# Second mixture of a recurrence and two mixtures of experts: program order on all engines, the input check and the loads spread over its blocks

## The chip, the core and the metric

The program runs on one core of a Trainium2 chip. The time is device microseconds of one execution; three runs of the kernel before gave 1580.2 us as their median (1580.01 to 1581.79). The engines are PE (TensorE matmul; PEld is its weight load), DVE (VectorE), ACT (ScalarE), POOL (GpSimd) and SP (SyncE, which here issues nearly all DMAs).

## The reference, cut to what is computed

```python
# 1. a recurrence over 768 steps, for 4 x 8 heads with a 40 x 40 state
for t in range(S):
    y[:, :, t] = einsum('bhd,bhde->bhe', rt, state)
    Sa = einsum('bhde,bhe->bhd', state, at)
    state = state * wt[:, :, None, :] - einsum('bhd,bhe->bhde', Sa, bt)
    state = state + einsum('bhd,bhe->bhde', vt, kt)
x = y.transpose(0, 2, 1, 3).reshape(3072, 320)
# 2. the first mixture, 1536 wide
x = ((x @ w_a) * (x @ w_b)) @ w_out
# 3. the second mixture, 4 experts, 1024 wide
p = domain_probs / (domain_probs.sum(-1, keepdims=True) + 1e-9)
for e in range(4):
    out += p[:, e:e+1] * (np.maximum(x @ w1[e], 0) @ w2[e])
```

## The kernel before

The program has one long straight run of instructions. The recurrence and the first mixture (class Moe1) are interleaved by hand up to about 853 us of the profile. The second mixture (class Moe2) follows, and this change is about it.

**Blocks.** The 3072 tokens are cut into 6 tiles t of 512. Each of the 4 experts e has 1024 hidden features, in 8 steps k of 128; two sets of weights u (512 features each) serve one expert. The list `steps` of `Moe2.run` runs over e, then t, then k: 192 blocks. Every fp32 operand is split into a high and a low part, so that three matmuls (high by high, high by low, low by high) replace one.

A block has two halves. `Moe2.l1` makes 8 matmuls of 512 columns (L719) into a PSUM tile l; then ACT makes hh, the relu of it rounded (L722), and DVE makes hl, the remainder (L723). `Moe2.l2` makes 12 matmuls of 320 columns (L736 to L738), three for each of the four 128-token groups o of the tile: L736 and L737 read hh, L738 reads hl. At k = 7 DVE adds the four groups o, weighted by the expert's probability, into the accumulator acc (L741); in the last expert the tile then goes to memory (L744). In the program l1 of block j + 1 stands ahead of l2 of block j.

**Loads.** `Moe2.loadx` fetches one token tile (6 DMAs, 768 KB, into a staging tile xB) and splits it: ACT casts each of three pieces to XH (L444), DVE subtracts to XL (L445). `Moe2.weights` fetches one set u (r1, 768 KB, L677, and r2, 640 KB, L679) and splits it: ACT casts, POOL subtracts (L445), and a third piece s goes through ACT and DVE (L687, L688). All staging tiles share one tag "st" with two buffers. The split weights have three buffers.

**The guard.** `Guard.run` checks the inputs of the recurrence while the second mixture runs: 48 chunks g of 419 KB are loaded (L795), ACT copies a part to gw (L797) and squares the rest with a sum (L801), DVE takes a maximum and a minimum of gw (L791). Then 24 parts gx of up to 512 KB of the first mixture's weights are squared by ACT (L810) and reduced by DVE. Its tag "g" has two buffers. `Moe2.run` calls it one step per block, in the program's text. `Guard.close` turns the results into one flag, and the program branches on it at its end to `general`, a slow path not taken here.

**Order.** Up to 853 us PE and SP stand in the order of the program's text. In the second mixture nothing is fixed by hand: a scheduler of the compiler orders each engine's instructions from the dependences, its own cost estimates and free buffers. Every engine then runs its instructions in the order given, and each waits for the semaphores of what it reads and overwrites.

Of the kernel before, what the change touches and what calls it, by code (L numbers as in the profile page):

```python
# [22 lines left out]
N = NPASS * NCH  # L23
# [3 lines left out]
DM = 320  # L27
FF1 = 1536
NE, FF2 = 4, 1024
# [48 lines left out]
class Att:  # L78
# [363 lines left out]
def split(nc, raw, hi, lo, eng):  # L442

    nc.scalar.copy(hi, raw)  # L444
    eng.tensor_tensor(out=lo, in0=raw, in1=hi, op=ALU.subtract)  # L445
# [5 lines left out]
class Moe1:  # L451
# [104 lines left out]
    def run(self):  # L556

        n = self.NK1
        blocks = [(t, i) for t in range(NT // 256) for i in range(n)]
        yield 0  # L560
        for t, i in blocks[:self.AHEAD]:
            yield from self.l1(t, i)
        for j, (t, i) in enumerate(blocks):
            if j + self.AHEAD < len(blocks):
                t1, i1 = blocks[j + self.AHEAD]
                if i1 == 0:
                    yield t1
                yield from self.l1(t1, i1)
            yield from self.l2(t, i)
# [73 lines left out]
class Moe2:  # L643


    TT, NB = 512, NT // 128
    NTT = NT // TT

# [23 lines left out]
        self.acc = self.fix2.tile([128, self.NB, DM], F32, name="acc")  # L672

    def weights(self, u, w1, w2):
        nc, pool = self.nc, self.pool
        r1 = pool.tile([128, 3, 512], F32, tag="st", name=f"r1_{u}")
        nc.sync.dma_start(r1[:], w1)  # L677
        r2 = pool.tile([128, 4, DM], F32, tag="st", name=f"r2_{u}")
        nc.sync.dma_start(r2[:], w2)  # L679
        h1 = pool.tile([128, 2, 512], F32R, tag="h1", name=f"h1_{u}", bufs=3)  # L680
        l1 = pool.tile([128, 2, 512], F32R, tag="l1", name=f"l1_{u}", bufs=3)
        s1 = pool.tile([128, 512], F32R, tag="s1", name=f"s1_{u}", bufs=3)
        h2 = pool.tile([128, 4, DM], F32R, tag="h2", name=f"h2_{u}", bufs=3)
        l2 = pool.tile([128, 4, DM], F32R, tag="l2", name=f"l2_{u}", bufs=3)
        for f in range(2):
            split(nc, r1[:, f], h1[:, f], l1[:, f], nc.gpsimd)
        nc.scalar.copy(s1[:], r1[:, 2])  # L687
        nc.vector.tensor_tensor(out=s1[64:128], in0=r1[64:128, 2], in1=s1[64:128], op=ALU.subtract)  # L688
        for q in range(2):
            k = slice(2 * q, 2 * q + 2)  # L690
            split(nc, r2[:, k], h2[:, k], l2[:, k], nc.gpsimd)
        self.W[u] = h1, l1, s1, h2, l2

    def loadx(self, t, fix):
        nc = self.nc
        XH = fix.tile([128, 3, self.TT], F32R, name=f"XH{t}")
        XL = fix.tile([128, 3, self.TT], F32R, name=f"XL{t}")
        xf = self.pool.tile([128, 3, self.TT], F32, tag="st", name=f"xB_{t}")
        for i in range(2):
            c, x = slice(256 * i, 256 * i + 256), self.x2d[2 * t + i]  # L700
            nc.sync.dma_start(xf[:, 0:2, c], x[:, 0:2])
            for z in range(2):
                nc.sync.dma_start(xf[64 * z:64 * z + 64, 2, c], x[:64, 2])
        for f in range(3):
            split(nc, xf[:, f], XH[:, f], XL[:, f], nc.vector)
        self.X[t] = XH, XL

    def l1(self, u, t, k, name):
        nc, TT = self.nc, self.TT
# [36 lines left out]
    def run(self, w1, w2, out, aside):  # L746

        nc = self.nc
        nc.gpsimd.memset(self.acc[:], 0.0)
        for t in range(1, self.NTT):  # L750
            self.loadx(t, self.fix2)
        steps = [(e, t, k) for e in range(NE) for t in range(self.NTT) for k in range(8)]

        def l1(j):
            e, t, k = steps[j]
            self.l1(2 * e + k // 4, t, k % 4, j)

        l1(0)
        for j, (e, t, k) in enumerate(steps):
            for z in range(2):  # L760
                if (t, k) == ((1, 0), (self.NTT - 1, 4))[z] and e + 1 < NE:
                    u = 2 * e + 2 + z
                    self.weights(u, w1[u], w2[u])
            if j + 1 < len(steps):
                l1(j + 1)
            self.l2(2 * e + k // 4, t, k % 4, j, self.pn[:, :, e], k == 0, k == 7, out if e == NE - 1 else None)
            next(aside, None)


class Guard:  # L770
# [15 lines left out]
    def run(self):  # L786
        nc, st, X = self.nc, self.st, mybir.AxisListType.X
        most, least, size, tiny = (st[:, i] for i in range(4))

        def worst(i, n, src, op):  # L790
            nc.vector.tensor_reduce(out=st[:src.shape[0], i, n:n + 1], in_=src, axis=X, op=op)  # L791

        for n in range(N):
            t = self.pool.tile([128, 1032], F32, tag="g", name=f"g_{n}")[:104]
            nc.sync.dma_start(t, self.e1[n])  # L795
            w = self.pool.tile([128, 256], F32, tag="w", name=f"gw_{n}")[:104]
            nc.scalar.copy(w.rearrange("p (a t) -> p a t", t=32), t[:, :264].rearrange("p (a t) -> p a t", t=33)[:, :, 1:])  # L797
            yield
            worst(0, n, w, ALU.max)
            worst(1, n, w, ALU.min)  # L800
            nc.scalar.activation(t, t, AF.Square, accum_out=size[:104, n:n + 1])  # L801
            yield
        n = 0
        for src in self.words:
            for i in range(0, src.shape[1], self.WORDS):
                m = min(self.WORDS, src.shape[1] - i)
                t = self.pool.tile([128, 1032], U32, tag="g", name=f"gx_{n}")[:, :m]
                nc.sync.dma_start(t, src[:, i:i + m])
                w = self.pool.tile([128, self.WORDS // 2], F32, tag="w", name=f"gy_{n}")[:, :m // 2]
                nc.scalar.activation(w, t.bitcast(F32).rearrange("p (n z) -> p n z", z=2)[:, :, 1], AF.Square)  # L810
                yield
                worst(3, n, w, ALU.min)
                n += 1
                yield

    def close(self, ps):

# [11 lines left out]
def general(tc, e1, e2, cst, wab, w2d, wo, probs, w1, w2, out):  # L829

    nc = tc.nc
    v = nc.vector
    NS = N // SUP
    with ExitStack() as c:
        dram = c.enter_context(tc.tile_pool(name="gdram", bufs=1, space=DRAM))
        x2 = dram.tile([NS, 128, 3, 256], F32, name="x2g")
        with ExitStack() as ctx:
# [5 lines left out]
            pool = ctx.enter_context(tc.tile_pool(name="grec", bufs=2))  # L843
# [19 lines left out]
            def tile4(name):  # L863
                return pool.tile(full, F32, tag=name, name=name)
# [4 lines left out]
            with tc.For_i(0, NS, 1) as s:  # L869
                ys = pool.tile([104, 8, SUP, 32], F32, tag="ys", name="gys", bufs=1)  # L870
                for step in range(2):
# [3 lines left out]
                    for z in range(2):  # L875
                        n = 2 * step + z
                        nc.sync.dma_start(E1[:, z], e1.rearrange("(s c) p m -> s c p m", c=SUP)[bass.ds(s, 1), n].rearrange("o p m -> p (o m)"))
                        src = e2.rearrange("(s c) p m -> s c p m", c=SUP)[bass.ds(s, 1), n].rearrange("o p m -> p (o m)")
                        src = src.rearrange("p (y v j t) -> p y v j t", y=2, v=2, j=4)
# [5 lines left out]
                    for z in range(2):  # L885
                        x = E1[:, z, 264:776].rearrange("p (a y t) -> p a y t", y=2, t=32)
                        for y in range(2):
                            nc.scalar.copy(kb[:, z, y], x[:, :, y])
                    w = E1[:, :, :264].rearrange("p z (a t) -> p z a t", t=33)[:, :, :, 1:]
                    a = E1[:, :, 776:].rearrange("p z (a t) -> p z a t", t=32)  # L890
                    for t in range(31, -1, -1):
                        dr, dv, x, y = (tile4(i) for i in ("gr", "gv", "gx", "gy"))
# [28 lines left out]
        m2 = Moe2(c, tc, x2, probs, None)  # L921
# [2 lines left out]
        nc.sync.dma_start(pd[:].rearrange("e p n -> p n e"), m2.pn[:])  # L924
        v.memset(m2.acc[:], 0.0)
        for t in range(m2.NTT):
            m2.loadx(t, m2.fix2)
        with tc.For_i(0, NE, 1) as e:
            for u in range(2):
                m2.weights(u, *(x.rearrange("(e u) p a b -> e u p a b", u=2)[bass.ds(e, 1), u].rearrange("o p a b -> (o p) a b") for x in (w1, w2)))  # L930
            p = m2.pool.tile([128, m2.NB], F32, tag="p", name="gp")
            nc.sync.dma_start(p[:], pd[bass.ds(e, 1)].rearrange("o p n -> (o p) n"))
            for t in range(m2.NTT):
                for k in range(8):
                    m2.l1(k // 4, t, k % 4, (t, k))
                    m2.l2(k // 4, t, k % 4, (t, k), p, k == 0, k == 7, None)
# [4 lines left out]
def body(ctx, tc, e1, e2, vt, cst, wab, w2d, wo, probs, w1, w2, out):  # L941
    nc = tc.nc
# [5 lines left out]
    with ExitStack() as ca:  # L948
# [41 lines left out]
        def whole(g):  # L990
            for _ in g:
                pass
# [10 lines left out]
        v, pool = nc.vector, nc.gpsimd  # L1003
# [126 lines left out]
        for n in range(SUP, N):  # L1130
            s, cc = divmod(n, SUP)
            m = n + LEAD
            g = (28, 20) if n < RING else (44, 28)
# [55 lines left out]
        hand.close()  # L1189
        cb.close()  # L1190
        m2 = Moe2(late, tc, x2d, probs, "right")
        m2.weights(0, w1[0], w2[0])
        m2.loadx(0, m2.fix)
        m2.weights(1, w1[1], w2[1])
        moe(1 << 20)
    m2.second()
    guard = Guard(late, tc, e1, (wab, w2d, wo))
    m2.run(w1, w2, out, guard.run())
    other = guard.close(m2.ps1.tile([128, 512], F32, tag="l1", name="other"))
    late.close()  # L1200
    with tc.If(other != 0):
# [53 lines left out]
```

## Time and profile before

| | |
|---|---|
| median of three runs | 1580.2 us |
| the profiled execution's own time | 1580.34 us |
| its span, first to last instruction | 1578.2 us |
| second mixture on PE | 853 to 1571 us of the span |
| busy over the span: PE, PEld, DVE, ACT, POOL | 90%, 82%, 53%, 37%, 27% |

The span is 2.1 us shorter than the execution's own time, and the profiled execution lies 0.1 us above the median. The page cuts the span into 40 slices of 39.5 us; the second mixture fills slices 22 to 40. From the row of PE alone they all look alike. The rows of PEld, ACT and of the DMAs differ between slices 22 to 27 (the guard's stretch, roughly 865 to 1075 us) and the rest.

### The profile page before, as it was taken

What the parts mean: (1) busy time and instruction counts of PE and PEld (TensorE: products, weight loads), DVE (VectorE), ACT (ScalarE), POOL (GpSimd) and SP (SyncE); (2) the same over time, 40 slices, a digit from 0 to 9 for tenths busy, and PEclk for the clock granted to TensorE, in tenths of its full rate; (3) what the DMA queues carried; (4) which work ended last, traced back from release to release, by engine and by line L of the source; (5) the groups of instructions that cost most, each with busy time, mean ns of one, the idle gap of its engine ahead of it and who ended that gap; (6) DMA issues with size and microseconds to landing.
All of it is one profiled execution on the core that took longest, in us unless ns stands there. A gap on an engine that the chain in (4) does not pass through costs nothing.

```text
span 1578.2 us, 40657 instructions
## 1 busy us (share of the span) xinstructions
PE 1427.1 (90%) x17202; PEld 1296.1 (82%) x17202; DVE 837.0 (53%) x1663; ACT 581.7 (37%) x1426; POOL 428.5 (27%) x810
## 2 busy tenths in 40 slices
PE   3455579999999999999999999999999999999998
PEld 2455568898898898898899877788999899989997
DVE  7658987777677677764445444553222322222222
ACT  2233334544544544543345766542112211121111
POOL 7083856246246246246013100020001100010000
PEclk9956679999999999999999999999999999999999
DMA  7745233443443443532124855671001100000001
GB/s 178 205 125 162 48 68 99 102 98 93 107 92 94 108 94 91 110 76 56 49 91 133 221 145 145 172 257 40 1 0 38 38 1 0 1 1 29 22 18 36
DMA packets 146850, 135.85 MB, mean 86 GB/s; under 512 B 98852, under 2 KB 116708, under 8 KB 146660
## 3 DMA queue, kind: packets, MB, share of 16 engines
q1 hardware_dynamic: 140468, 124.72, 30.4%
q10 hardware_dynamic: 6192, 8.45, 1.7%
q8 instruction: 137, 2.24, 0.6%
q14 instruction: 53, 0.43, 0.1%
HBM read 115.03 MB, written 18.09 MB: 84 GB/s over the span
## 4 chain that ended last, share of the span: by engine, by line


## 5 line engine op out<-in xcount | busy, mean ns | idle before, releaser
L723 DVE SCALAR_TENSOR_TENSOR hl<-l,hh 128x512 fp32r<-128x512 f32 x192 | 132.3, 689 | 344.1 <-ACT hh L722 344.0
L586 PE MATMUL l<-xh,w 128*128 128x256 f32 x1440 | 293.7, 289 | 12.1 <-DVE g L590 6.5
L722 ACT ACTIVATE hh<-l 128x512 fp32r<-128x512 f32 x192 | 114.0, 594 | 396.6 <-PE l L719 396.5
L586 PE MATMUL l<-xl,w 128*128 128x256 f32 x864 | 246.1, 292 | 5.9 <-DVE xl L445 5.7
L586 PEld LDWEIGHTS l<-xh,w 128*128 128x128 f32 x1440 | 237.7, 194 | 15.5 <-DVE g L590 7.1
L736 PE MATMUL o<-h,hh 128*128 128x320 f32 x768 | 238.9, 311 | 9.2 <-ACT hh L722 5.8
L738 PE MATMUL o<-h,hl 128*128 128x320 f32 x768 | 239.6, 313 | 4.6 <-DVE hl L723 4.5
L737 PE MATMUL o<-l,hh 128*128 128x320 f32 x768 | 236.9, 309 | 0.0
L218 POOL TENSOR_TENSOR tmp<-tblk,xblk 128x126 f32<-128x126 f32 (+22 forms) x341 | 141.1, 414 | 269.9 <-DMA tblk<-td 164.3
L445 POOL TENSOR_TENSOR l<-r,h 128x512 fp32r<-128x512 f32 (+1 forms) x32 | 47.0, 1490 | 577.5 <-ACT h L444 577.5
L586 PEld LDWEIGHTS l<-xl,w 128*128 128x128 f32 x864 | 167.6, 194 | 9.9 <-DVE xl L445 8.2
L736 PEld LDWEIGHTS o<-h,hh 128*128 128x128 f32 x768 | 144.2, 188 | 25.6 <-ACT hh L722 13.6
L221 POOL TENSOR_TENSOR xblk<-xblk,tmp 128x126 f32<-128x126 f32 (+22 forms) x341 | 152.0, 446 | 26.7
L738 PEld LDWEIGHTS o<-h,hl 128*128 128x128 f32 x768 | 144.0, 188 | 11.3 <-DVE hl L723 11.0
L719 PE MATMUL l<-XL,h 128*128 128x512 f32 x384 | 151.7, 395 | 0.0
L719 PE MATMUL l<-XH,h 128*128 128x512 f32 x384 | 151.6, 395 | 0.0
L719 PE MATMUL l<-XH,l 128*128 128x512 f32 x384 | 149.9, 390 | 0.0
L737 PEld LDWEIGHTS o<-l,hh 128*128 128x128 f32 x768 | 144.2, 188 | 6.7
L597 ACT CAST gh<-g 128x256 fp32r<-128x256 f32 x144 | 58.4, 406 | 157.4 <-DVE g L590 153.4
L174 PE MATMUL psT<-A,e 40*64 40x32 f32 x1472 | 63.6, 240 | 39.8 <-POOL A L154 12.3
L588 ACT COPY a<-l 128x256 f32<-128x256 f32 x144 | 53.5, 372 | 123.0 <-PE l L586 121.7
L174 PEld LDWEIGHTS psT<-A,e 40*64 40x64 f32 x1472 | 58.0, 158 | 43.6 <-issue 24.0
(122 smaller groups left out, 2628.0 us busy)
## 6 DMA issues: line engine op xcount, KB each, us to landing
g<-e SPq DMA_DIRECT2D x48, 419.2 KB
e<-e SPq DMA_DIRECT2D x46, 419.2 KB
e<-e SPq DMA_DIRECT2D x48, 208.0 KB
tblk<-td SPq DMA_DIRECT2D x96, 64.0 KB
r<-w SPq DMA_DIRECT2D x8, 768.0 KB
gx<-wab SPq DMA_DIRECT2D x12, 512.0 KB
r<-w SPq DMA_DIRECT2D x8, 640.0 KB
G<-vt SPq DMA_DIRECT2D x96, 52.0 KB
```

The costliest lines, as they stand in the source:

```text
L174: nc.tensor.matmul(T[P][KROW[P]:KROW[P] + 64, a], ke[r, a].rearrange("p y t -> p (y t)"), self.A[P][r, k, a], start=True, stop=True)
L218: eng.tensor_tensor(out=t, in0=tb[:, k + 1:, k:k + 1].to_broadcast([128, m, c]), in1=X[:, k:k + 1, :c].to_broadcast([128, m, c]), op=ALU.mult)
L221: eng.tensor_tensor(out=X[:, k + 1:, :c], in0=X[:, k + 1:, :c], in1=t, op=ALU.subtract)
L586: nc.tensor.matmul(o, l, r, start=j == 0, stop=j == len(ops) - 1)
L588: nc.scalar.copy(a[:], ps[:, 0:256])
L597: self.nc.scalar.copy(gh[:], g[:])
L719: nc.tensor.matmul(ps[:], l, r, start=i == 0, stop=i == len(ops) - 1)
L722: nc.scalar.activation(hh[:], ps[:], AF.Relu)
L723: nc.vector.scalar_tensor_tensor(out=hl[:], in0=ps[:], scalar=0.0, in1=hh[:], op0=ALU.max, op1=ALU.subtract)
L736: nc.tensor.matmul(o[:], hh[:, s], h2[:, k], start=first, stop=False)
L737: nc.tensor.matmul(o[:], hh[:, s], lo2[:, k], start=False, stop=False)
L738: nc.tensor.matmul(o[:], hl[:, s], h2[:, k], start=False, stop=last)
```

## The change

The diff, cut to its core. `LAND` is the number of blocks between the issue of a load and the first instruction that reads it. `weights` and `loadx` become generators, which are advanced one step after each block; `whole` runs one to its end at once, for the first two sets of weights and the first token tile. The slow path `general` does the same in loops and is left out here.

```diff
+    LAND = 3
...
     def weights(self, u, w1, w2):
-        r1 = pool.tile([128, 3, 512], F32, tag="st", name=f"r1_{u}")
+        r1 = pool.tile([128, 3, 512], F32, tag="st", name=f"r1_{u}", bufs=4)
...
+        for _ in range(self.LAND):
+            yield
         for f in range(2):
             split(nc, r1[:, f], h1[:, f], l1[:, f], nc.gpsimd)
+            yield
         nc.scalar.copy(s1[:], r1[:, 2])
...
         for q in range(2):
+            yield
             k = slice(2 * q, 2 * q + 2)
             split(nc, r2[:, k], h2[:, k], l2[:, k], nc.gpsimd)
...
     def loadx(self, t, fix):
...
+        for _ in range(self.LAND):
+            yield
         for f in range(3):
             split(nc, xf[:, f], XH[:, f], XL[:, f], nc.vector)
+            yield
...
     def run(self, w1, w2, out, aside):
-        for t in range(1, self.NTT):
-            self.loadx(t, self.fix2)
         steps = [(e, t, k) for e in range(NE) for t in range(self.NTT) for k in range(8)]
+        begin = {8 * t - 8: [self.loadx(t, self.fix2)] for t in range(1, self.NTT)}
+        for e in range(NE - 1):
+            for z in range(2):
+                u = 2 * e + 2 + z
+                begin[8 * self.NTT * (e + 1) - 8 + 4 * z] = [self.weights(u, w1[u], w2[u])]
...
+        going = []
         l1(0)
         for j, (e, t, k) in enumerate(steps):
-            for z in range(2):
-                if (t, k) == ((1, 0), (self.NTT - 1, 4))[z] and e + 1 < NE:
-                    u = 2 * e + 2 + z
-                    self.weights(u, w1[u], w2[u])
+            going += begin.pop(j, [])
             if j + 1 < len(steps):
                 l1(j + 1)
             self.l2(2 * e + k // 4, t, k % 4, j, self.pn[:, :, e], k == 0, k == 7, out if e == NE - 1 else None)
-            next(aside, None)
+            going = [g for g in going if next(g, going) is not going]
+            if j >= 8:
+                next(aside, None)
...
+        def chunk(n):
             t = self.pool.tile([128, 1032], F32, tag="g", name=f"g_{n}")[:104]
             nc.sync.dma_start(t, self.e1[n])
+            yield
             w = self.pool.tile([128, 256], F32, tag="w", name=f"gw_{n}")[:104]
             nc.scalar.copy(w.rearrange("p (a t) -> p a t", t=32), t[:, :264].rearrange("p (a t) -> p a t", t=33)[:, :, 1:])
             yield
             worst(0, n, w, ALU.max)
             worst(1, n, w, ALU.min)
             nc.scalar.activation(t, t, AF.Square, accum_out=size[:104, n:n + 1])
...
+        jobs = [chunk(n) for n in range(N)] + [part(n, src) for n, src in enumerate(parts)]
+        next(jobs[0])
+        for i, job in enumerate(jobs):
+            if i + 1 < len(jobs):
+                next(jobs[i + 1])
+            for _ in job:
+                yield
+            yield
...
-    m2.run(w1, w2, out, guard.run())
+    with tc.manual_schedule(engines={getattr(mybir.EngineType, x) for x in ("PE", "SP", "DVE", "Pool", "Activation")}):
+        m2.run(w1, w2, out, guard.run())
```

So `run` now stands on all five engines in the order of its text. Token tile t is issued at block 8t - 8 and split at blocks 8t - 5 to 8t - 3; its first reader is l1 in block 8t - 1's turn. The weights of the next expert are issued 8 and 4 blocks before its first block and split over five turns from the third on. The guard starts at block 8, takes two blocks for each chunk or part, and issues each load two blocks before its copy; 72 chunks and parts take 144 blocks.

The order on ACT where the guard runs, before: `g_15` is chunk 15 of the guard and `gw_15` its copied part, `hh_16` is the relu of block 16.

```order
L797 COPY gw_15_15620<-g_15_15618 104x256
L801 ACTIVATE g_15_15618,gst_14596<-g_15_15618 104x1032
L722 ACTIVATE hh_16_15159<-l1_16_15150 128x512
L797 COPY gw_16_15685<-g_16_15683 104x256
L801 ACTIVATE g_16_15683,gst_14596<-g_16_15683 104x1032
L797 COPY gw_17_15742<-g_17_15740 104x256
L722 ACTIVATE hh_17_15191<-l1_17_15182 128x512
L801 ACTIVATE g_17_15740,gst_14596<-g_17_15740 104x1032
L797 COPY gw_18_15799<-g_18_15797 104x256
L801 ACTIVATE g_18_15797,gst_14596<-g_18_15797 104x1032
```

The same blocks on ACT now:

```order
L731 ACTIVATE hh_15_15042<-l1_15_15033 128x512
L810 COPY gw_3_15060<-g_3_14999 104x256
L731 ACTIVATE hh_16_15071<-l1_16_15062 128x512
L814 ACTIVATE g_3_14999,gst_14596<-g_3_14999 104x1032
L731 ACTIVATE hh_17_15103<-l1_17_15094 128x512
L810 COPY gw_4_15134<-g_4_15058 104x256
L731 ACTIVATE hh_18_15145<-l1_18_15136 128x512
```

Between two relus stood two or three of the guard's instructions, chunk 15 and on at block 16; now one stands there, and chunk 3 is at hand.

The order on ACT where the second mixture begins, before: `x2_11` is the last result tile of the first mixture, `XH1` and `XH2` are the split token tiles 1 and 2, `hh_0` the first relu.

```order
L636 COPY x2_11_14569<-o01_11_14242 128x512
L637 COPY x2_11_14569<-o2_11_14243 64x256
L444 CAST XH1_14603<-xB_1_14605 128x512 x3
L444 CAST XH2_14618<-xB_2_14620 128x512 x3
L722 ACTIVATE hh_0_14687<-l1_0_14678 128x512
```

The same place now:

```order
L636 COPY x2_11_14569<-o01_11_14242 128x512
L637 COPY x2_11_14569<-o2_11_14243 64x256
L731 ACTIVATE hh_0_14614<-l1_0_14605 128x512
L731 ACTIVATE hh_1_14627<-l1_1_14618 128x512
L731 ACTIVATE hh_2_14665<-l1_2_14656 128x512
```

The six casts that stood ahead of the first relu have moved behind it, to blocks 3 to 5 and 11 to 13.

The order of DMA issues on SP where the next expert's weights `r1_2`, `r2_2` stand, before:

```order
L795 DMA g_2_14834<-e1 104x1032
L677 DMA r1_2_14927<-w1 128x1536
L795 DMA g_3_14891<-e1 104x1032
L679 DMA r2_2_14929<-w2 128x1280
L795 DMA g_4_14975<-e1 104x1032
```

And now:

```order
L807 DMA g_16_15811<-e1 104x1032
L679 DMA r1_2_15876<-w1 128x1536
L681 DMA r2_2_15878<-w2 128x1280
L807 DMA g_17_15885<-e1 104x1032
L807 DMA g_18_15942<-e1 104x1032
```

The weights have moved back from the guard's third chunk (L795) to its seventeenth (now L807), and one set's two transfers stand together.

## Rows read from the trace of the kernel before

**Rows 1.** Page: two engines' busy tenths in 40 slices of the span.

```profile
PE   3455579999999999999999999999999999999998
PEld 2455568898898898898899877788999899989997
```

**Rows 2.** Stretches: PE, PEld, DVE, ACT, POOL busy (count), PEclk, DMA share, GB/s.

```profile
870.00:1063.00 193.00, 179.47 (x930) 149.80 (x929) 95.32 (x194) 118.63 (x227) 17.43 (x12) 1.00 0.65 185
...
1083.00:1276.00 193.00, 193.00 (x1073) 174.55 (x1072) 52.02 (x83) 37.58 (x64) 11.32 (x8) 1.00 0.05 16
```

**Rows 3.** Waits in 870 to 1063: total us, times, longest us.

```profile
ACT gw L797 <- DMA g<-e: 48.5, 46, 2.4
...
PEld o L736 <- ACT hh L722: 13.1, 18, 1.2
PEld o L738 <- DVE hl L723: 10.5, 24, 0.6
```

**Rows 4.** Waits in 1083 to 1560, first row of the same view.

```profile
ACT hh L722 <- PE l L719: 376.5, 129, 3.0
```

**Rows 5.** Timeline in the guard's stretch: start us, us, engine, operation [idle before].

```profile
933.13 0.41 ACT L797 COPY gw<-g 104x256 f32<-104x256 f32 x1 [1.52 <-DMA g<-e]
...
933.57 1.07 ACT L801 ACTIVATE g<-g 104x1032 f32<-104x1032 f32 x1
...
935.58 0.41 ACT L797 COPY gw<-g 104x256 f32<-104x256 f32 x1 [0.85 <-DMA g<-e]
...
936.02 1.07 ACT L801 ACTIVATE g<-g 104x1032 f32<-104x1032 f32 x1
...
937.08 0.58 ACT L722 ACTIVATE hh<-l 128x512 fp32r<-128x512 f32 x1
...
937.71 0.41 PE L736 MATMUL o<-h,hh 128*128 128x320 f32 x1 [0.41 <-ACT hh L722]
...
938.44 0.41 PE L738 MATMUL o<-h,hl 128*128 128x320 f32 x1 [0.17 <-DVE hl L723]
```

**Rows 6.** Timeline, one undisturbed block after the guard, ACT, DVE and PE.

```profile
1149.88 0.60 ACT L722 ACTIVATE hh<-l 128x512 fp32r<-128x512 f32 x1 [2.99 <-PE l L719]
...
1150.51 0.69 DVE L723 SCALAR_TENSOR_TENSOR hl<-l,hh 128x512 fp32r<-128x512 f32 x1 [2.90 <-ACT hh L722]
...
1153.27 0.30 PE L736 MATMUL o<-h,hh 128*128 128x320 f32 x1
...
1153.56 0.31 PE L738 MATMUL o<-h,hl 128*128 128x320 f32 x1
```

**Rows 7.** Timeline of SP's queue, issues of two loads.

```profile
830.11 0.35 SPq L679 DMA_DIRECT2D r<-w  x1
...
864.72 0.50 SPq L795 DMA_DIRECT2D g<-e  x1
```

**Rows 8.** Timeline of ACT, the first instructions that read those loads.

```profile
834.60 1.36 ACT L444 CAST h<-r 128x640 fp32r<-128x640 f32 x2 [0.40 <-DMA r<-w]
...
869.64 0.41 ACT L797 COPY gw<-g 104x256 f32<-104x256 f32 x1 [2.42 <-DMA g<-e]
```

**Rows 9.** Timeline, all engines, the first blocks of the second mixture.

```profile
854.48 0.47 SPq L640 DMA_DIRECT2D x<-x  x1
...
856.80 0.39 PE L719 MATMUL l<-XH,h 128*128 128x512 f32 x1
...
857.28 1.09 ACT L722 ACTIVATE hh<-l 128x512 fp32r<-128x512 f32 x2
...
857.93 0.41 PE L736 MATMUL o<-h,hh 128*128 128x320 f32 x1
```

**Rows 10.** Groups in 870 to 1063: count | busy us, mean ns | idle before.

```profile
L791 DVE TENSOR_REDUCE gst<-gw 104x1 f32<-104x256 f32 x96 | 35.8, 414 | 55.1 <-ACT gw L797 54.9
...
L741 DVE SCALAR_TENSOR_TENSOR acc<-o,pn,acc 128x320 f32<-128x320 f32 x24 | 11.8, 542 | 0.0
```

**Rows 11.** Timeline of PE, the larger of two waits late in the first mixture.

```profile
833.81 0.38 PE L586 MATMUL l<-xh,w 128*128 128x256 f32 x1 [0.22 <-DVE g L590]
```

More of the change, by code (lines that the diff above doesn't have):

```diff
@@ L675, in weights @@
         nc, pool = self.nc, self.pool
-        r1 = pool.tile([128, 3, 512], F32, tag="st", name=f"r1_{u}")
+        r1 = pool.tile([128, 3, 512], F32, tag="st", name=f"r1_{u}", bufs=4)
         nc.sync.dma_start(r1[:], w1)
-        r2 = pool.tile([128, 4, DM], F32, tag="st", name=f"r2_{u}")
+        r2 = pool.tile([128, 4, DM], F32, tag="st", name=f"r2_{u}", bufs=4)
         nc.sync.dma_start(r2[:], w2)
@@ L684, in weights @@
         l2 = pool.tile([128, 4, DM], F32R, tag="l2", name=f"l2_{u}", bufs=3)
+        for _ in range(self.LAND):
+            yield
         for f in range(2):
             split(nc, r1[:, f], h1[:, f], l1[:, f], nc.gpsimd)
+            yield
         nc.scalar.copy(s1[:], r1[:, 2])
         nc.vector.tensor_tensor(out=s1[64:128], in0=r1[64:128, 2], in1=s1[64:128], op=ALU.subtract)
+        self.W[u] = h1, l1, s1, h2, l2
         for q in range(2):
+            yield
             k = slice(2 * q, 2 * q + 2)
             split(nc, r2[:, k], h2[:, k], l2[:, k], nc.gpsimd)
-        self.W[u] = h1, l1, s1, h2, l2
     def loadx(self, t, fix):
@@ L697, in loadx @@
         XL = fix.tile([128, 3, self.TT], F32R, name=f"XL{t}")
-        xf = self.pool.tile([128, 3, self.TT], F32, tag="st", name=f"xB_{t}")
+        xf = self.pool.tile([128, 3, self.TT], F32, tag="st", name=f"xB_{t}", bufs=4)
         for i in range(2):
@@ L703, in loadx @@
                 nc.sync.dma_start(xf[64 * z:64 * z + 64, 2, c], x[:64, 2])
+        self.X[t] = XH, XL
+        for _ in range(self.LAND):
+            yield
         for f in range(3):
             split(nc, xf[:, f], XH[:, f], XL[:, f], nc.vector)
-        self.X[t] = XH, XL
+            yield
     def l1(self, u, t, k, name):
@@ L791, in worst @@
             nc.vector.tensor_reduce(out=st[:src.shape[0], i, n:n + 1], in_=src, axis=X, op=op)
-        for n in range(N):
+        def chunk(n):
             t = self.pool.tile([128, 1032], F32, tag="g", name=f"g_{n}")[:104]
             nc.sync.dma_start(t, self.e1[n])
+            yield
             w = self.pool.tile([128, 256], F32, tag="w", name=f"gw_{n}")[:104]
@@ L801, in run, with part @@
             nc.scalar.activation(t, t, AF.Square, accum_out=size[:104, n:n + 1])
+        def part(n, src):
+            t = self.pool.tile([128, 1032], U32, tag="g", name=f"gx_{n}")[:, :src.shape[1]]
+            nc.sync.dma_start(t, src)
             yield
[L803 to L810, printed above, removed]
+            w = self.pool.tile([128, self.WORDS // 2], F32, tag="w", name=f"gy_{n}")[:, :src.shape[1] // 2]
+            nc.scalar.activation(w, t.bitcast(F32).rearrange("p (n z) -> p n z", z=2)[:, :, 1], AF.Square)
+            yield
+            worst(3, n, w, ALU.min)
+        parts = [src[:, i:min(i + self.WORDS, src.shape[1])] for src in self.words for i in range(0, src.shape[1], self.WORDS)]
+        jobs = [chunk(n) for n in range(N)] + [part(n, src) for n, src in enumerate(parts)]
[4 more added lines that the diff above has]
+            for _ in job:
                 yield
-                worst(3, n, w, ALU.min)
-                n += 1
-                yield
+            yield
     def close(self, ps):
@@ L926, in general @@
         for t in range(m2.NTT):
-            m2.loadx(t, m2.fix2)
+            for _ in m2.loadx(t, m2.fix2):
+                pass
         with tc.For_i(0, NE, 1) as e:
             for u in range(2):
-                m2.weights(u, *(x.rearrange("(e u) p a b -> e u p a b", u=2)[bass.ds(e, 1), u].rearrange("o p a b -> (o p) a b") for x in (w1, w2)))
+                for _ in m2.weights(u, *(x.rearrange("(e u) p a b -> e u p a b", u=2)[bass.ds(e, 1), u].rearrange("o p a b -> (o p) a b") for x in (w1, w2))):
+                    pass
             p = m2.pool.tile([128, m2.NB], F32, tag="p", name="gp")
@@ L1191, in body @@
         m2 = Moe2(late, tc, x2d, probs, "right")
-        m2.weights(0, w1[0], w2[0])
-        m2.loadx(0, m2.fix)
-        m2.weights(1, w1[1], w2[1])
+        whole(m2.weights(0, w1[0], w2[0]))
+        whole(m2.loadx(0, m2.fix))
+        whole(m2.weights(1, w1[1], w2[1]))
         moe(1 << 20)
```

## The prediction

> **What bounds the kernel now.** I read the page first. In its slices PE shows nines from the seventh slice to the last but one, so by that row the second mixture is full everywhere; PEld falls to 7 in slices 24 to 26 [rows 1]. So I cut the second mixture into two stretches of the same 193 us and counted matmuls: 930 from 870 to 1063, 1073 from 1083 to 1276 [rows 2]. Both run the same 20 matmuls per block, at a granted clock of 1.00, its 2.4 GHz level. The second stretch takes 193 / 1073 = 0.180 us for one, 3.60 us for a block. At that pace 930 matmuls take 930 x 0.180 = 167.3 us, so the first stretch loses **25.7 us**.
>
> The view of waits says where. In the first stretch weight loads wait for the relu hh on ACT 13.1 us and for hl on DVE 10.5 us, together 23.6 of the 25.7 us; ACT itself waits 48.5 us, in 46 places, for the guard's loads [rows 3]. In 1083 to 1560 the longest entry is the other way round, ACT waits for PE [rows 4]; no entry of that view has PE waiting. The timeline shows the mechanism: from 933.13 to 937.08 ACT does two copies and two squares of the guard, with a wait of 0.85 us for a load between them, and only then the relu; PE waits for that relu and, 0.7 us later, for hl [rows 5]. ACT is not full there (118.6 of 193 us, [rows 2]); it is in the wrong order, since a copy that has to wait for a load stands ahead of a relu.
>
> PE's idle time alone would size this wrongly: 193 - 179.5 = 13.5 us [rows 2]. The Trainium skill, Perfetto Trace Analysis, section Identifying the Most-Contended Engine, says that matmul busy time is no measure of headroom and that the busy time of weight loads is. By that rule the loss would be (174.55 - 149.80) / 0.904 = 27.4 us and the time 1.7 us lower than mine; the trace sides with it against the 13.5 us, since the count gives 25.7.
>
> **The change, part by part.**
>
> *The guard spread out.* Work is the same; it is done over 144 blocks (some 518 us) instead of about 200 us. In the worst block ACT has the relu 0.60, a square 1.07 with its short read-out, and one cast; its sum is about 0.6 + 1.1 + 0.7 = 2.4 us of the 3.60 [rows 5, 6], the cast being half of a pair of 1.36 [rows 8]. The wait that the change adds is the copy's on its load, and behind it on ACT stand the next relu, then hl on DVE, then PE. Its cover: a load can be issued when the square two jobs earlier is through, and its copy comes three blocks later, less the square: 3 x 3.60 - 1.2 = 9.6 us. The guard's load took 4.9 us from issue (864.72) to the copy that waited for it (869.64) [rows 7, 8]. Past 9.6 us ACT waits, but uses first its own idle 2.99 - 0.41 = 2.6 us before the next relu, then the margin of hl: done at 1151.20, read at 1153.56, 2.36 us [rows 6]. So a load may take 9.6 + 2.6 + 2.4 = 14.6 us before PE feels it. I take 0 for these waits.
>
> *Weights and token tiles.* They are issued three turns, 10.8 us, ahead of their first cast. A 640 KB load took 4.5 us, from 830.11 to 834.60 [rows 7, 8]; behind a 768 KB one at the same rate 4.5 x 2.2 = 9.9 us, but r2 is first read after two more turns. A guard load that follows a whole set on SP is held by its buffer for two blocks anyway. SP itself is held by nothing else: four staging buffers instead of two mean that no issue waits for a split. For both together I take **+0.5 us** of new waits, between 0 (rows above) and 6 us (one us lost at each of the six weight sets, which would need loads three times as long).
>
> *DVE at a tile's end.* hl 0.69, four additions to acc of 0.54 [rows 6, 10] and two reductions of 0.41 make 3.7 us in one block of 3.60, with a lighter one before and after; the next hl slips by under 1 us, against 2.36 of margin. The first group o is free some 0.7 + 0.54 us after hl begins, and its next writer comes after eight more matmuls, so it costs nothing. If that cover were gone, each tile's end would lose up to 0.5 us (a rival below).
>
> *The order of PE.* In the undisturbed stretch the built order of PE was l1 of one block, l2 of the one before, as it is now written. So from there to the end nothing changes, and the last block and the output keep their place.
>
> *The beginning.* The first relu waits for the store of the first mixture's last tile, whose memory it takes (issued 854.48); it ran at 857.28, behind six casts, and PE began l2 at 857.93 [rows 9]. The casts are gone from there, the store is not. Before, PE filled the time from 856.80 with four matmuls of block 2; written in the text's order it has nothing to fill with. The loss is up to 857.93 - 856.80 = 1.1 us, and 0.2 more for hl. If the store lands early, there is a gain of 0.3. I take **+0.8 us**, between -0.3 and +1.3, since the relu began right at the casts' end and the store is the nearer bound.
>
> *The end of the first mixture.* Four staging buffers let the loads of the first two weight sets go out earlier, and on ACT the casts of the first token tile move up by two instructions. PE waits twice there, 0.22 us the longer [rows 11]. I take 0, between -1 and +1.
>
> The sum, on the profiled execution: 1578.2 - 25.7 + 0.5 + 0.8 = 1553.8 us of span, with the 2.1 us around it 1555.9; the median lies 0.1 us lower: **1555.8 us**.
>
> **The rivals.**
>
> *Loads at the expert's change.* ACT stands in the text's order behind a load that is late, because guard, r1 and r2 share one queue. For it: the stretch of before moves 185 GB/s at a DMA share of 0.65 [rows 2], so loads there are already slowed by each other. Against it: the new traffic is one guard load of 0.43 MB in 7.2 us and six sets more, far less. One us for each of six sets: 1561.8.
>
> *DVE at tile ends.* The 3.7 us in a block of 3.60 eat the margin. For it: DVE in order cannot put hl ahead of acc. Against: 2.36 us [rows 6]. At 18 tile ends with guard work, 0.5 us each: 1555.8 + 9 = 1564.8.
>
> *No change.* The slow pace belongs to the DMA traffic or to shared memory, not to the order, and the guard carries it along into later blocks. For it: only the stretch with traffic is slow. Against: the two waits on ACT and DVE already hold 23.6 of 25.7 us [rows 3]. Time: 1580.
>
> *Slower.* The guard's loop on ACT closes on itself: square, issue, landing, copy, next square. Once a load takes over 14.6 us, every further us is lost in each round of two jobs, 36 rounds. From 15.3 us the whole gain is given back, at 16 us the time is 1555.8 + 36 x 1.4 = 1606. Against it: 4.9 us [rows 7, 8].
>
> **How the numbers follow.** Forecast 0.73, loads 0.12, DVE 0.06, no change 0.05, slower 0.04. The range takes the bounds of the sum: at the low end no new waits (-0.5), the beginning at -0.3 (-1.1), the end of the first mixture at -1 and about a us of small waits just outside the stretch, 1552; at the high end 6 us of new waits (+5.5), the beginning at +1.3 (+0.5) and +1, 1563. That holds the forecast and most of the first rival, some 0.83. A measurement of this kernel tells about 0.2% (3 us) from no change: faster 0.91, within it 0.05, slower 0.04.
>
> **What would show it.** Right: in the new trace a stretch of 193 us from 870 on has about 1073 matmuls and over 174 us of weight loads; ACT waits for the guard's loads in no block after the first; the guard's last reduction lies near block 152, about 1400 us; PE still waits about a us at its first l2. Wrong: waits of PE for hh around 1000 to 1026, 1172 to 1198 or 1345 to 1371 (loads at the expert's change); for hl or o every eighth block (DVE); a matmul pace below 0.180 us each without waits (traffic); copies of the guard that wait each time (the loop).

## The result and the profile after

| | before | after |
|---|---|---|
| median, five runs each | 1581.8 us (1580.0 to 1583.2) | 1556.3 us (1554.1 to 1558.4) |
| profiled execution | 1580.3 us | 1556.4 us |
| its span | 1578.2 us | 1554.6 us |

The ratio is 0.9832, with a 95% interval from 0.9815 to 0.9849. The change makes the kernel faster by some 1.7%; the forecast was 1555.8 us.

The page of after has no sevens left in the row of PEld after the first slices but for the last one, where [rows 1] had a dip in slices 24 to 26:

```profile
PE   3445679999999999999999999999999999999998
PEld 2444569998998998998899899999999999999997
```

The two stretches of [rows 2], now of after (busy us and count of PE, PEld, DVE, ACT and POOL, then the granted clock, the DMA share and GB/s):

```profile
870.00:1063.00 193.00, 193.00 (x1075) 174.68 (x1074) 76.38 (x147) 78.08 (x152) 11.46 (x8) 1.00 0.30 81
1083.00:1276.00 193.00, 193.00 (x1076) 174.79 (x1075) 69.25 (x135) 69.40 (x133) 11.46 (x8) 1.00 0.28 81
```

They have become alike. The first went from 930 matmuls to 1075, and ACT's 118.6 us of work there became 78.1, with most of the rest in the second stretch (37.6 before, 69.4 now).

The waits of the whole second mixture, 853 to 1555 us (total us, times, longest us):

```profile
ACT hh L731 <- PE l L728: 469.6, 190, 3.9
...
ACT hh L731 <- DMA x<-x: 2.6, 1, 2.6
...
PEld o L745 <- ACT hh L731: 0.8, 1, 0.8
...
PEld o L747 <- DVE hl L732: 0.4, 1, 0.4
PE o L745 <- ACT hh L731: 0.3, 1, 0.3
...
PE o L747 <- DVE hl L732: 0.2, 1, 0.2
```

The relu's line is now L731, the three matmul lines of l2 are L745 to L747. What [rows 3] held is gone: no entry has ACT waiting for a load of the guard, where there were 48.5 us. The waits of PE for hh and hl that are left have the count 1 each, and all four are at the first l2. ACT waits for PE, as in [rows 4] in the undisturbed part.

ACT's timeline in the same part of the program as [rows 5] (start us, us, engine, operation, idle before):

```profile
928.25 0.60 ACT L731 ACTIVATE hh<-l 128x512 fp32r<-128x512 f32 x1 [2.70 <-PE l L728]
928.75 0.61 ACT L444 CAST XH<-xB 128x512 fp32r<-128x512 f32 x1
929.25 1.07 ACT L814 ACTIVATE g<-g 104x1032 f32<-104x1032 f32 x1
...
931.85 0.60 ACT L731 ACTIVATE hh<-l 128x512 fp32r<-128x512 f32 x1 [1.43 <-PE l L728]
932.34 0.61 ACT L444 CAST XH<-xB 128x512 fp32r<-128x512 f32 x1
932.85 0.41 ACT L810 COPY gw<-g 104x256 f32<-104x256 f32 x1
```

One guard instruction and one cast stand between two relus, and the copy at 932.85 has no idle time before it: its load had landed. The relus follow each other in 3.60 us.

**The second mixture alone.** The first matmul of the second mixture and its last one bound the changed part. For before and for after they are, in PE's timeline:

```profile
853.05 0.40 PE L719 MATMUL l<-XH,h 128*128 128x512 f32 x1
...
1570.51 0.31 PE L738 MATMUL o<-h,hl 128*128 128x320 f32 x1
```

```profile
854.78 0.40 PE L728 MATMUL l<-XH,h 128*128 128x512 f32 x1
...
1546.84 0.31 PE L747 MATMUL o<-h,hl 128*128 128x320 f32 x1
```

From one to the other it is 717.46 us before and 692.06 after, so the change is worth 25.40 us there. The tail behind it is 7.7 us in both. The part ahead came out 1.7 us later, which gives the span's 23.6. That part hardly differs in any kernel of this study, yet its end lies between 851.3 and 855.7 us over eleven profiled executions; so single us of the whole time say little, and the experiments are read by this distance, called the **PE distance** below.

| kernel | PE distance | time | ratio to before, 95% |
|---|---|---|---|
| before | 717.46 us | 1581.8 us | 1 |
| after | 692.06 | 1556.3 | 0.9832 (0.9815 to 0.9849) |
| e1, before's text in fixed order | 708.45 | 1570.2 | 0.9935 (0.9912 to 0.9959) |
| e2, after's text without fixed order | 717.46 | 1580.1 | 0.9991 (0.9979 to 1.0003) |
| e3, before without the guard | 691.27 | 1557.5 | 0.9855 (0.9832 to 0.9878) |
| e4, LAND = 0 | 691.97 | 1555.6 | 0.9832 (0.9803 to 0.9860) |
| e5, two guard steps per block | 692.05 | 1554.0 | 0.9822 (0.9793 to 0.9850) |
| e6, three guard steps per block | 730.13 | 1592.9 | 1.0067 (1.0040 to 1.0094) |
| e7, one guard buffer | 692.06 | 1556.8 | 0.9839 (0.9811 to 0.9868) |
| e8, l1 two blocks ahead | 690.99 | 1554.2 | 0.9835 (0.9806 to 0.9863) |
| e9, one buffer and two steps | 803.55 | 1664.8 | one run |

Each ratio is taken against runs of before from the same round, whose medians are 1581.8 (after), 1581.2 (e1, e2, e3, e8) and 1582.2 us (e4 to e7).

### The profile page after: what moved, and what is told of

Read it like the earlier page. It is cut to its first block, busy times and chain, and to the rows that moved or that the text cites. A ratio compares the mean times of both kernels' runs of the same rounds, so it can differ in the third digit from the quotient of the medians.

```text
span 1554.6 us, 40653 instructions
## 1 busy us (share of the span) xinstructions
PE 1416.2 (91%) x17202; PEld 1299.7 (84%) x17202; DVE 830.4 (53%) x1663; ACT 574.3 (37%) x1426; POOL 424.6 (27%) x810
## 4 chain that ended last, share of the span: by engine, by line
## 5 line engine op out<-in xcount | busy, mean ns | idle before, releaser
L731 ACT ACTIVATE hh<-l 128x512 fp32r<-128x512 f32 x192 | 114.9, 599 | 472.2 <-PE l L728 469.6
L586 PEld LDWEIGHTS l<-xh,w 128*128 128x128 f32 x1440 | 240.3, 196 | 14.6 <-ACT xh L444 6.3
L747 PE MATMUL o<-h,hl 128*128 128x320 f32 x768 | 237.3, 309 | 0.2 <-DVE hl L732 0.2
L745 PE MATMUL o<-h,hh 128*128 128x320 f32 x768 | 236.6, 308 | 0.3 <-ACT hh L731 0.3
L221 POOL TENSOR_TENSOR xblk<-xblk,tmp 128x126 f32<-128x126 f32 (+22 forms) x341 | 148.5, 435 | 26.7
L745 PEld LDWEIGHTS o<-h,hh 128*128 128x128 f32 x768 | 144.2, 188 | 8.3 <-ACT hh L731 0.8
L747 PEld LDWEIGHTS o<-h,hl 128*128 128x128 f32 x768 | 144.2, 188 | 0.4 <-DVE hl L732 0.4
```

The costliest lines, as they stand in the source:

```text
L221: eng.tensor_tensor(out=X[:, k + 1:, :c], in0=X[:, k + 1:, :c], in1=t, op=ALU.subtract)
L586: nc.tensor.matmul(o, l, r, start=j == 0, stop=j == len(ops) - 1)
L731: nc.scalar.activation(hh[:], ps[:], AF.Relu)
L745: nc.tensor.matmul(o[:], hh[:, s], h2[:, k], start=first, stop=False)
L747: nc.tensor.matmul(o[:], hl[:, s], h2[:, k], start=False, stop=last)
```

## The experiments

The theory: the 25 us were lost because copies that wait for loads stood ahead of relus on ACT, and the new order ends that. Its rivals: the loss belongs to the guard's traffic and density of work; the gain comes from one part of the change alone (the fixed order, or the text that spreads the work); the longer leads of the loads do it.

### Is it the guard? Before without it

```diff
-    m2.run(w1, w2, out, guard.run())
+    m2.run(w1, w2, out, iter(()))
```

> The kernel before with the guard's loads, copies, squares and reductions left out (the flag is made from preset values); token tiles and weights are loaded in the same bunches as before. My theory: the guard alone made the 25.7 us of waits in the stretch from 870 to 1063; what is left is one to two us around the first relu. Time 1580 - 25 = 1555 (1554 to 1558), and the stretch holds about 1073 matmuls. Rival, the casts of token tiles and weights in bunches made half of it: 1565 to 1570, with waits of PE left near 860 to 890 and at the second set of weights.

Measured: 1557.5 us, PE distance 691.27 us. The first stretch:

```profile
870.00:1063.00 193.00, 193.00 (x1075) 174.78 (x1074) 55.52 (x88) 41.88 (x71) 17.43 (x12) 1.00 0.09 29
```

With no guard at all, before's order of everything else runs 1075 matmuls there, as many as after does with the guard. So the whole loss, 717.46 - 691.27 = 26.2 us, hung on the guard, and after hides its work completely: the 0.8 us by which the PE distance of after is longer are its longer waits at the first l2. (This kernel's tail behind the last matmul takes 9.6 us instead of 7.7, so its whole time is no shorter than that of after.)

### The fixed order alone

```diff
-    m2.run(w1, w2, out, guard.run())
+    with tc.manual_schedule(engines={getattr(mybir.EngineType, x) for x in ("PE", "SP", "DVE", "Pool", "Activation")}):
+        m2.run(w1, w2, out, guard.run())
```

This is the text of before, and only its order is held.

> The text of before (all token tiles loaded ahead of block 0, weights in one piece, the guard's load in the step of its copy), with the order of the text fixed on all five engines for the second mixture. My theory: the 25 us were lost because copies and squares of the guard, pulled forward in a bunch, stood ahead of relus. Fixed order spreads the guard over two blocks for each chunk here as well, so the middle loses nothing; but fifteen casts of token tiles 1 to 5 now stand ahead of the first relu on ACT, and the last of them needs a load that ended about 872 us of the span before, so PE waits some 15 us at its first l2. Time 1556 + 15 = 1571. Rival one, the fixed order is all of the gain: 1556 to 1558. Rival two, the spread loads and splits are what counts and order alone gives nothing: 1578 to 1582.

Measured: 1570.2 us, close to the theory's 1571. Before's text asks for the split of all five further token tiles ahead of the first block. ACT's timeline (rows of one line with x6 or x2 are that many instructions; fifteen casts stand before the relu):

```profile
852.31 3.23 ACT L444 CAST XH<-xB 128x512 fp32r<-128x512 f32 x6
859.69 1.14 ACT L444 CAST XH<-xB 128x512 fp32r<-128x512 f32 x2 [4.16 <-DMA xB<-x]
...
869.63 1.08 ACT L722 ACTIVATE hh<-l 128x512 fp32r<-128x512 f32 x2
```

and the waits of PEld, of which the other two entries are 0.2 us each:

```profile
PEld o L736 <- ACT hh L722: 15.5, 1, 15.5
```

The first l2 in PE's timeline:

```profile
870.28 0.64 PE L736 MATMUL o<-h,hh 128*128 128x320 f32 x1 [15.02 <-ACT hh L722]
```

PE waits once and never again, the guard's stretch included: holding the order of even the old text removes the guard's waits, since that text gives the guard one step per block. What it costs is one block of casts that wait for loads with a relu behind them. The moved casts of the change are therefore a needed part, worth 708.45 - 692.06 = 16.4 us.

### The spread text alone

```diff
-    with tc.manual_schedule(engines={getattr(mybir.EngineType, x) for x in ("PE", "SP", "DVE", "Pool", "Activation")}):
-        m2.run(w1, w2, out, guard.run())
+    m2.run(w1, w2, out, guard.run())
```

> The changed kernel's text, without the fixed order: the scheduler orders all engines in the second mixture. My theory: the guard's steps are what has to be apart, and the text already puts a chunk's copy two blocks behind its load, so that the scheduler has no copy ready to pull ahead; PE waits under 2 us in all, time 1555 to 1558. Rival, the fixed order is needed: the scheduler bunches guard work as before, PE loses 10 to 25 us in the first 200 us of the second mixture, time 1566 to 1580.

Measured: 1580.1 us in ten runs, a PE distance of 717.46 us, to the hundredth that of before. Here my theory fell. I had held that the text, once parted by yields, would carry the order by itself. The stretch and its waits are those of before:

```profile
870.00:1063.00 193.00, 180.24 (x928) 151.04 (x927) 94.34 (x189) 115.09 (x219) 16.96 (x12) 0.99 0.65 191
```

```profile
ACT gw L810 <- DMA g<-e: 45.6, 41, 2.4
...
PEld o L745 <- ACT hh L731: 13.8, 17, 2.0
PEld o L747 <- DVE hl L732: 9.1, 22, 0.6
```

ACT's timeline between two relus:

```profile
935.29 0.58 ACT L731 ACTIVATE hh<-l 128x512 fp32r<-128x512 f32 x1
936.39 0.41 ACT L810 COPY gw<-g 104x256 f32<-104x256 f32 x1 [0.52 <-DMA g<-e]
936.83 1.07 ACT L814 ACTIVATE g<-g 104x1032 f32<-104x1032 f32 x1
...
939.74 0.41 ACT L810 COPY gw<-g 104x256 f32<-104x256 f32 x1 [1.75 <-DMA g<-e]
940.18 1.06 ACT L814 ACTIVATE g<-g 104x1032 f32<-104x1032 f32 x1
...
941.24 0.57 ACT L731 ACTIVATE hh<-l 128x512 fp32r<-128x512 f32 x1
```

The scheduler pulls the guard's chunks together again, up to two copies and squares to a relu; the yields in the text did not keep them apart. So neither part suffices: the fixed order alone gives 9.0 us on the PE distance, the text alone nothing, both together 25.4. All five engines are held at once, and no run holds the order of ACT alone. That it is ACT's order that counts, and not that of SP or PE, is read from the waits; no run of its own shows it.

### Density or order? Two and three guard steps per block

```diff
-            if j >= 8:
+            for _ in range(2 if j >= 8 else 0):
                 next(aside, None)
```

and the same with 3.

> The changed kernel with two guard steps in a block: a chunk per block, 80 percent of the density that the guard had before (48 chunks in 142 us), and its order kept, one copy and one square between two relus. ACT has 0.6 + 0.41 + 1.07 + at most 0.7 in a block of 3.6 us; a load has two blocks less the copy and the square, about 5.5 us, against 4.9. My theory, the place of the guard's instructions and not their density cost the time: PE waits under 2 us in all, 1555 to 1558. Rival, density: 0.8 of the 25 us come back, 1572 to 1578.

Measured with two steps: 1554.0 us, PE distance 692.05 us. The stretch:

```profile
870.00:1063.00 193.00, 193.00 (x1072) 174.44 (x1071) 92.61 (x198) 115.03 (x223) 11.47 (x8) 1.00 0.49 138
```

ACT works 115.0 of the 193 us, as much as in the variant just above (115.1), and PE loses nothing. So the amount of ACT's work was not the cause, as the prediction read from [rows 2]. The guard's pace here is one chunk per block, against some 1.2 in before (48 chunks in 142 us, 39.6 blocks of 3.59 us). No run holds the order at that pace, so whether a held order alone would do there stays open. The DMA share is 0.49, not 0.65, so this run does not by itself clear the traffic at 0.65 either. PE's own timeline of before does so for PE: within l1 its matmuls start 0.231 us apart in the median and at most 0.240, in the stretch with a share of 0.65 as in the one with 0.05. Traffic thus did not slow the matmuls themselves; that it lengthened the loads that ACT waits for is not excluded.

> The changed kernel with three guard steps in a block: a chunk and a half per block. With two buffers two chunks cannot come faster than a load, a copy and a square, 4.9 + 0.4 + 1.1 = 6.4 us, so 3.2 us each or less if loads overlap better (2.96 us each in the kernel before); three steps in order then need 4.4 to 4.8 us in a block of 3.6 for 48 blocks. My theory, ACT in the text's order waits for loads and PE with it: 0.8 to 1.2 us lost in each of 48 blocks, 1590 to 1615, slower than the kernel before, with the waits spread evenly from block 8 to 56. Rival, margins absorb it: under 1565.

Measured with three steps: 1592.9 us, slower than before, inside the expected range. The waits in 870 to 1063:

```profile
DVE hl L732 <- ACT hh L731: 81.7, 40, 5.5
ACT gw L810 <- DMA g<-e: 47.4, 38, 3.9
...
PEld o L745 <- ACT hh L731: 18.7, 14, 3.7
```

Now copies wait for loads 47.4 us, nearly the 48.5 of [rows 3], and in a fixed order nothing can step past them. The expectation that the loss would spread evenly was wrong: blocks ran from 3.59 us, no loss, to 8.4 us in the same stretch. The loss recurs with the token tile of eight blocks: of the 38.6 us over the pace of 3.59, 30.7 lie ahead of l2 in the first, third and fourth block of a tile. Why these blocks are hit is open. The run shows where the cover of the new order ends: between two and three steps per block.

### What hides the loads

Two kernels take parts of the cover away. `LAND` is the lead that the change gives weights and token tiles:

```diff
-    LAND = 3
+    LAND = 0
```

> The changed kernel with LAND = 0: each token tile's and weight set's first cast stands on ACT in the turn in which the load is issued in the text. My theory: SP runs ahead of the text; all that holds it is the guard's buffer, so a load goes out when the square three turns earlier is through and still has 3 x 3.6 - 1.2 = 9.6 us to land, against 4.5 to 5 us. ACT waits for no token tile or weight load for longer than 1 us, PE for none: 1555 to 1558. Rival, the three blocks of lead are what hides the loads: a cast waits some 4 us for each of five token tiles and six sets, in order ahead of the next relu; past the margin of 2.4 us PE loses about 2 us for each, 1575 to 1580.

Measured: 1555.6 us, PE distance 691.97 us, no wait of ACT for a load other than the 2.6 us for the store at the beginning. With a text that puts no block between issue and cast, nothing is late either. In both kernels SP issues the pair r1, r2 of the fourth set at 1009 us; the first cast of it follows some 20 us later in after and still some 9 us later here. So the lead that counts is SP's own: it runs ahead of the other engines until a buffer of the guard holds it (SP waits 326.8 us for the guard's squares in both). `LAND` = 3 is harmless and buys nothing here.

One staging buffer for the guard instead of two:

```diff
-            t = self.pool.tile([128, 1032], F32, tag="g", name=f"g_{n}")[:104]
+            t = self.pool.tile([128, 1032], F32, tag="g", name=f"g_{n}", bufs=1)[:104]
...
-            t = self.pool.tile([128, 1032], U32, tag="g", name=f"gx_{n}")[:, :src.shape[1]]
+            t = self.pool.tile([128, 1032], U32, tag="g", name=f"gx_{n}", bufs=1)[:, :src.shape[1]]
```

> The changed kernel with one buffer in place of two for the guard's loads. A load can go out only when the square of the job before is through and its copy comes one block later: 3.6 - 1.2 = 2.4 us against 4.9. My theory, by the sum of the prediction: ACT waits some 2.5 us for each of 72 loads (180 us in all), but this fits into its idle time ahead of the next relu (2.6 us) and the margin of hl (2.4 us), so PE waits under 2 us in all: 1555 to 1558. Rival, a wait in order on ACT reaches PE: 2.5 us x 72, above 1700.

Measured: 1556.8 us, and a PE distance of 692.06 us, that of after. ACT's waits and PEld's:

```profile
ACT hh L731 <- PE l L728: 382.6, 185, 3.9
ACT gw L810 <- DMA g<-e: 80.9, 47, 2.5
```

```profile
PEld o L745 <- ACT hh L731: 0.7, 1, 0.7
PEld o L747 <- DVE hl L732: 0.4, 1, 0.4
```

ACT now waits for every chunk, 1.7 us in the mean and 80.9 us in all (I had expected some 180), more than in before, and PE feels none of it. A long row of waits on ACT is thus no loss in itself; it depends on whether the waits and the work between two relus fit into a block. Of the two margins that the prediction counted on, this is clear evidence for the first, ACT's idle time before the next relu: 185 of the 192 relus still waited for PE. The second, the margin of hl, was hardly needed.

### The closed loop: one buffer and two steps

One buffer and two steps per block together: each load can go out only when the square before it is done, and its copy is due one block later.

> After, with one staging buffer for the guard instead of two and two guard steps per block instead of one, so that a load can be issued only when the square of the job before it is through, and its copy stands one block behind that square. This builds the closed loop of the slower rival on purpose. In the run with one buffer alone, some 4.4 us went by from a square's end to the next copy's begin (931.26 to 935.68). Theory of the loop: issue and landing 4.4, copy 0.41, square 1.07 and the relu or cast that stand between them 0.6 make about 6.4 us per block in place of 3.59, over 72 blocks: about 1556 + 72 x 2.8 = 1758 us, between 1700 and 1800, with a wait of PE for hh in nearly all of these blocks. Rival: ACT's idle time and the margin of hl absorb it as they did with one buffer alone: under 1565 us.

Measured: 1664.8 us. The loop is there, but the size was missed by nearly a half. ACT's timeline:

```profile
927.21 0.18 ACT L814 ACTIVATION_READ_ACCUMULATOR g<-g 104x1 f32 x1
927.30 0.58 ACT L731 ACTIVATE hh<-l 128x512 fp32r<-128x512 f32 x1
932.01 0.41 ACT L810 COPY gw<-g 104x256 f32<-104x256 f32 x1 [4.13 <-DMA g<-e]
932.44 1.06 ACT L814 ACTIVATE g<-g 104x1032 f32<-104x1032 f32 x1
```

The relu runs while the load is under way, so its 0.6 us do not belong to the loop. Over the 45 blocks from 898.0 to 1155.2 us a block took 257.2 / 45 = 5.72 us instead of 6.4; the 24 blocks after them, in which the 23 loads gx and one pass of ACT over each fall, took 102.6 / 24 = 4.28. That is 45 x 2.13 + 24 x 0.69 = 112 us, against a PE distance longer by 111.5. From a square's end to the next copy it took 3.8 to 5.1 us here, 4.2 in the median. The copies wait 149.3 us for loads in the first 45 blocks, 44 times, 3.4 us in the mean: here a single wait between two relus is enough to cost time, since with the copy and the square it is longer than the block.

### The beginning

```diff
         l1(0)
+        l1(1)
...
-            if j + 1 < len(steps):
-                l1(j + 1)
+            if j + 2 < len(steps):
+                l1(j + 2)
```

> The changed kernel with l1 two blocks ahead of l2 in place of one, from the first block on. My theory: the only waits left on PE stand at the first l2 (0.71 + 0.47 and small ones, about 1.1 us in the profile of the changed kernel), behind the first relu, which waits for the store of the first mixture's last tile; two tiles of l1 in front of it hide them. First l2 after 48 matmuls of 512 columns instead of 16, no wait, time 1555.2 against 1556.3, a difference too small for the timing and to be read in the trace. Rival, the deeper lead makes later blocks wait for their weights or their PSUM tile: over 2 us of waits of PE at the changes of expert, time above 1558.

Measured: 1554.2 us. Three tiles of l1 stand ahead of the first l2, which are 24 matmuls and not the 48 that the expectation names. PE waits for neither hh nor hl anywhere in the second mixture, and the PE distance is 690.99 us, 1.07 under that of after. As a time it cannot be told from after (the intervals overlap), but on PE's own rows it is the shortest of all kernels here with the guard's work in them.

## Why the prediction was right, point by point

- **The stretch that loses 25.7 us.** Right in place and size. The PE distance fell by 25.40 us; with the 0.7 that the beginning added, 26.1 were recovered. The count of matmuls (25.7) came nearest; PE's idle time gave 13.5. The Trainium skill, Perfetto Trace Analysis, section Identifying the Most-Contended Engine, judges by MFU (the share of the peak matmul rate that is used) and by the busy time of weight loads in place of matmul busy time. The trace agrees with it: the busy time of weight loads gave 27.4, and the count, which for equal blocks measures what MFU does, 25.7.
- **No wait for the guard's loads.** Right: no entry after, and with one buffer ACT's idle time took 1.7 us at each chunk. No run made a load as slow as the 14.6 us that the prediction names as the limit, so that number is not tested.
- **New waits +0.5 us.** They were 0. The lead of three turns by which I argued them away is not what does it (`LAND` = 0 changes nothing); SP's run ahead is.
- **DVE at tile ends, 0.** Right: PE waits for hl once, at the first l2, and never at a tile's end.
- **The beginning +0.8 us.** Right: after has these rows of PE, and of ACT the relu that waits for the store:

```profile
858.29 0.40 PE L728 MATMUL l<-XL,s 128*128 128x512 f32 x1
859.00 0.41 PE L745 MATMUL o<-h,hh 128*128 128x320 f32 x1 [0.32 <-ACT hh L731]
859.25 0.31 PE L746 MATMUL o<-l,hh 128*128 128x320 f32 x1
859.73 0.41 PE L747 MATMUL o<-h,hl 128*128 128x320 f32 x1 [0.17 <-DVE hl L732]
```

```profile
858.35 1.09 ACT L731 ACTIVATE hh<-l 128x512 fp32r<-128x512 f32 x2 [2.62 <-DMA x<-x]
```

  Starts that otherwise lie 0.23 and 0.15 us apart are 0.71, 0.25 and 0.48 apart, and one more 0.25: together about 1.0 us over the pace, against 0.3 before [rows 9], so +0.7. The bound chosen was the right one, the store. That l1 a block further ahead covers it was not among the prediction's ideas; e8 shows it.
- **The end of the first mixture, 0.** The part from 805 us to the first matmul of the second mixture took 0.6 us less, inside the bounds; one pair of executions does not tell whether the change did it.
- **The sum.** It came out 0.5 us under the median, partly by luck: the second mixture gained 25.4 us, not 24.4, and the part ahead of it came 1.7 us later by chance.
- **The rivals.** Loads at the expert's change and DVE at tile ends left no row. Where relus come late the second one exists: PE waits for acc twice in before's stretch (3.2 us) and nine times in e9 (17.2 us). No change: this is what the text without the fixed order gives (1580 us); its order and its DMA share (0.65) are both those of before, and PE's matmul pace speaks against traffic as the direct reason. Slower by the closed loop: the mechanism exists, at the price e9 shows, but needs one buffer and two steps per block, or three steps, to begin.
- **What would show it.** 1075 matmuls and 174.7 us of weight loads in the stretch (1073 and over 174 were named). The guard's last reductions, at L803, end near 1400 us as foreseen. The row counts 23 parts gx where the prediction reckoned with 24, so the guard takes 71 jobs and 142 blocks:

```profile
L803 DVE TENSOR_REDUCE gst<-gy x23: 409/676/689, 1239.2 to 1397.5; 128x1 f32<-128x512 f32 x22, 128x1 f32<-128x256 f32 x1
```

What the prediction didn't see is that it rested on one line. The order listing showed it the result of fixed order and spread text together, so it could not go wrong there, but its words give the credit to the spreading.

## What to carry to other kernels

Look for what stands between two links of the critical chain in the queue of an engine that is not full: what counts is whether the waits and the work there, taken together, fit between the two. A copy that waited 1.7 us cost nothing (e7), a copy and a square with hardly a wait cost nothing (e5), and both with a wait of 3.4 us in the mean cost 2.1 us in every block (e9). Where a scheduler sets the order, a text that parts the work may change nothing until the order is held, and holding the order makes every early block of loads and casts in that text count as written. Time the changed stage on the bounding engine from its first to its last instruction: four kernels here agree in it within 0.1 us, while their whole times differ by 3.

## What the runs showed of the hardware

**A long wait of PE costs more than its length.** In e1 PE's last matmul before the wait started at 854.86, and it resumed at 870.28. The stretches (columns as above; the granted clock is the third figure from the end):

```profile
856.00:858.00 2.00, 0.00 (x0) 0.00 (x0) 0.88 (x2) 0.00 (x0) 2.00 (x1) 0.95 0.77 202
858.00:860.00 2.00, 0.00 (x0) 0.00 (x0) 0.00 (x0) 0.31 (x1) 0.09 (x1) 0.50 0.73 207
...
872.00:874.00 2.00, 2.00 (x9) 2.00 (x9) 0.00 (x0) 0.00 (x0) 0.00 (x0) 0.50 0.00 0
874.00:875.00 1.00, 1.00 (x4) 0.77 (x3) 0.00 (x0) 0.00 (x0) 0.00 (x0) 0.57 0.00 0
875.00:876.00 1.00, 1.00 (x6) 0.80 (x5) 0.00 (x0) 0.00 (x0) 0.00 (x0) 1.00 0.00 0
```

The granted clock fell to 0.50, the 1.2 GHz level, while PE was idle, and stayed there until 874.9 with PE busy. The fifteen matmuls from 870.28 to 875.02 took 4.74 us; at the pace of after's rows (0.147 and 0.233 us) they take 12 x 0.147 + 3 x 0.233 = 2.5. So 2.3 us came on top of 15.2 us of waiting, and both, less the 1.0 us that after loses at the same place, come to 16.5 us, against the 16.4 of the PE distance. In e9 PE was busy for 0.47 us from 920 to 923; from 923 to 926.5 the granted clock was 0.51, and from 926.5 to 930 it was 1.00 again. Its mean from 898 to 1155 us was 0.93.

**Blocks of 3.63 us.** In before, after and the variants the eight blocks with token tile 0 take 3.63 us instead of 3.59, for each expert, without any wait. Tile 0's split tiles lie in another pool than the others'. Why that would matter is open; it is 1.3 us in all.
